# A decode kernel of two attention layers: six more V blocks kept in PSUM between the layers, and a new order in layer 2

## The chip, the cores and the metric

The kernel runs on one core of a Trainium2 chip. Its engines are TensorE (PE, whose weight loads are listed as PEld), VectorE (DVE), ScalarE (ACT), GpSimd (POOL) and SyncE (SP, which here only issues DMAs); 16 DMA engines carry the transfers. SBUF is the on-chip memory that DMAs fill; PSUM is the memory that TensorE writes, eight banks of 512 float32 words a partition here. The metric is the device time of one execution in microseconds (us). A second table is the hardware profiler's record of one execution of the same program.

## What is computed

One token (`x`, 640 values) goes twice through the same two blocks, A (attention) and B (an MLP with mixing), with the same weights and the same caches both times:

```python
x = x + A(layernorm(x));  x = x + B(layernorm(x))      # layer 1
x = x + A(layernorm(x));  x = x + B(layernorm(x))      # layer 2

def A(x):                       # 32 heads of 192, the last W = 4096 rows of each cache
    q = x @ wq
    p = softmax(q @ k.T * 192 ** -0.5)       # per head, [4096]
    return (p @ v) @ wo

def B(x):                       # one position: the shifted parts are zero
    return x + gelu(layernorm(x) @ w3) @ w4
```

With one position, the shifts in B push their content out, so that `w1` and `w2` have no effect on the result. K and V of a head are 4096 x 192 in bfloat16, 1536 KB each. Both layers use the same K, V and `wo`.

## The kernel before

**Cells.** Head data lives in twelve cells of SBUF, each 6144 bfloat16 words on 128 partitions, one K or V of a head. `take` (L147) hands out the cell that has been free longest, `give` (L152) returns one. A load into a cell waits until its last user is done, so the order of `give` sets when SP can issue which load. A V is 32 blocks of 192 words a partition, each block one key position a partition.

**The stream.** `layer_stream` (L247) writes down the loads of a layer in order; `need` issues them up to the one asked for. For each group of four heads the stream has K of the next group and V of the current one in turn, then `wo` of an earlier group; at the end of a layer come w3 and w4. All loads go through SP's queue, each of them also waiting for the eighth before it to land.

**What is kept for layer 2.** Layer 1 takes the groups from the last heads to the first. So the heads 0 to 7 come last and the transposed K of these eight stay in their cells (`kept`), as do V 3 (`VC`) and `wo` 0. V 2 (`VP`) is kept in pieces: 20 blocks are moved by `v_words` (L629) with VectorE transposes into four banks of PSUM (`V_bank`), since no cell is free, and moved back in layer 2 when one is; the other 12 blocks lie behind `wo` 0 in its cell. Of V 4 (`VX`), 24 blocks lie in the two spare areas `kl` and `kx`, so that layer 2 loads only 8 of its 32 blocks, 384 KB. `v_pair` (L185) tells where a pair of blocks lies.

**The work of a group** (`attention`, L720). VectorE transposes K in four quarters (`transpose_quart`, L433; `T` asks for two), TensorE makes scores (`scores`, L524, `S`). For a whole group the softmax runs in steps (`softmax_steps`, L551): maximum, turn, exponentials on ScalarE, `turn_p` on VectorE, `swap` on TensorE, which turns the probabilities into a PSUM tile and ScalarE copies them to `PT`. `pv` (L639) multiplies with V into `O_ps` and VectorE transposes the result; `o_fold` sums it up. `out_proj` or `out_row` (L670, L687) apply `wo` of the group before, `qproj_steps` make the next group's queries. The order of instructions on PE, DVE, ACT and SP is the order in which this code calls them (`manual_schedule`).

**Small results** (sums, turned maxima, queries) go to tiles of the pool `psm`, two PSUM banks in turn, each tile one bank; `ps` of the new version takes over this call. `mixer` (L963) makes block B, its 12 columns of hidden values in a free part of `V_bank` and of `O_bank` (`h_ps`).

Of the kernel before, what the change touches and what calls it, by code (L numbers as in the profile page):

```python
# [59 lines left out]
def kernel(  # L60
# [46 lines left out]
    VC, VP, VX, VW, VN = 3, 2, 4, 20 * Dh // 2, (NKL + NKX) * Dh  # L107
# [21 lines left out]
    psV = ctx.enter_context(tc.tile_pool(name="psV", bufs=1, space=PSUM))  # L129

# [38 lines left out]
    def load_v(layer, h):  # L169
        t = take(("v", layer, h))  # L170
        src = A_v_cache[0, h, s0:Sk, :].rearrange("(p j) d -> p (j d)", p=P)
        cut = (2 * VW,) if h == VP else (FREE - VN, FREE - NKX * Dh) if h == VX else ()
        if h in GROUPS[layer][-1][-1 - layer:]:
            cut = FREE // 2,
        i = 0
        for e in cut + (FREE,):
            kept_v = h == VP or h == VX and i > 0
            if not cut:
                load(t[:], src, layer == 0 or h >= 2)
            elif layer == 0 or not kept_v:  # L180
                nc.sync.dma_start(v_pair(t, h, i, e - i), src[:, i:e])
            i = e
        return t

    def v_pair(V, h, i, n):  # L185

        if h == VP and i >= 2 * VW:
            V, i = loaded["wo", 0, 0], i - 2 * VW + NA * D
        elif h == VX and i >= FREE - NKX * Dh:
            V, i = kx, i - (FREE - NKX * Dh)  # L190
        elif h == VX and i >= FREE - VN:
            V, i = kl, i - (FREE - VN)
        return V[:, i:i + n]

# [184 lines left out]
    warm_ps = psm.tile([32, 32], F32, tag="psm")  # L379
# [6 lines left out]
    xT_ps = psm.tile([P, ND], F32, tag="psm")  # L386
# [6 lines left out]
    def ln_center(x, rowsum):  # L393

        mean_ps = psm.tile([P, 1], F32, tag="psm")
# [11 lines left out]
        def total():  # L407
            var_ps = psm.tile([P, 1], F32, tag="psm")
            nc.tensor.matmul(var_ps[:], lhsT=ones, rhs=ssq[:, 0:1], start=True, stop=True)
            return var_ps  # L410
# [44 lines left out]
    def qproj_steps(c, xc, part=None, row=None):  # L455
# [6 lines left out]
        def project():  # L462
            need("wq", 0, ND - 1)
            if row is not None:
                N = QC // 2
                qr_ps = psm.tile([33, N], F32, tag="psm")
# [9 lines left out]
            qT_ps = psm.tile([P, n], F32, tag="psm")  # L476
# [8 lines left out]
        def spread():  # L485
            if row is not None:
                qT_ps = psm.tile([P, n], F32, tag="psm")
                for tl in range(n):
                    i, j = divmod(tl, n // 2)
                    nc.tensor.matmul(qT_ps[:, tl:tl + 1], lhsT=row[:, j * P:(j + 1) * P],  # L490
                                     rhs=Eq[0:33, i, 0:1], start=True, stop=True)
                held["q"] = qT_ps
# [6 lines left out]
        def repeat():  # L499
            Qrep_ps = psm.tile([P, 4 * n], F32, tag="psm")  # L500
# [50 lines left out]
    def softmax_steps(n, ST_ps, sc, space):  # L551
# [8 lines left out]
        def turn_max():  # L560
            pmT_ps = psm.tile([1, P], F32, tag="psm")
# [16 lines left out]
        def spread_max():  # L578
            nb_ps = psm.tile([P, 1], F32, tag="psm")
# [16 lines left out]
        def swap():  # L596
            ng = NGK // NT
            PT_ps = psm.tile([P, n, NJ4, NGK], F32, tag="psm")
# [7 lines left out]
            l_ps = psm.tile([P, QH], F32, tag="psm")  # L606
# [20 lines left out]
    h_ps = V_bank[:, VW:VW + NF // 2], O_bank[:, 2 * Dh:2 * Dh + NF // 2]  # L627

    def v_words(layer):  # L629

        V = need("v", layer, VP)
        step = 512
        for i in range(0, VW, step):
            n = min(step, VW - i)
            a = V[:, 2 * i:2 * (i + n)].bitcast(U32)
            b = V_bank[:, i:i + n].bitcast(U32)
            nc.vector.transpose(b if layer == 0 else a, a if layer == 0 else b)

    def pv(layer, h, hq, PT, mid=None):  # L639
        V = need("v", layer, h)  # L640
        if (layer, h) == (0, VP):
            v_words(0)
# [10 lines left out]
        else:  # L653
            give(("v", layer, h))
        nc.vector.transpose(o_sb[:], O_ps.rearrange("p (e a c) -> p e c a", e=2, c=NA))  # L655

    def o_fold(h, oT, rl, add=False):
        r = slice(32 * (h % QH), 32 * (h % QH) + 32)
        oT_ps = psm.tile([P, NA], F32, tag="psm")
# [10 lines left out]
    def out_proj(layer, *terms):  # L670

        y_ps = psm.tile([P, ND], F32, tag="psm")
# [14 lines left out]
    def out_row(layer, c, oT, acc, first):  # L687
# [3 lines left out]
        yr_ps = psm.tile([33, N], F32, tag="psm")  # L691
# [16 lines left out]
    def turn_row(acc):  # L708
        y_ps = psm.tile([P, ND], F32, tag="psm")
# [10 lines left out]
    def attention(layer, x_cur, rs_cur, x_new, z_new, rs_new, ss_new):  # L720
# [29 lines left out]
        def add_y(y_ps, n):  # L750
            y_new = x_new if n == 0 else short("y_acc", ND)
            if n == 1:
# [5 lines left out]
                def center():  # L758
                    nm_ps = psm.tile([P, 1], F32, tag="psm")
# [53 lines left out]
        for gi, cur in enumerate(groups):  # L813
# [6 lines left out]
            if nxt:  # L820
                part_max, turn_max, full_max, spread_max, turn_p, swap, recip = softmax_steps(len(cur), ST, sc, o_words)
# [24 lines left out]
                else:  # L846
# [18 lines left out]
                    in_row = gi - 1 in rows  # L865
                    if pending is not None:
                        y_ps = out_row(layer, *pending, acc, gi - 1 == rows[0]) if in_row else out_proj(layer, pending)
                    turn_p()
                    if quick:
                        y_ps()  # L870
# [4 lines left out]
                    if in_row:  # L875
                        if not quick:
                            y_ps()
                            if gi - 1 == rows[-1]:
                                add_y(turn_row(acc), 2)
# [4 lines left out]
                    PT = swap()  # L884
# [12 lines left out]
            for hq, h in order:  # L897
# [4 lines left out]
                elif quick and hq == 2:  # L902
                    T(h3, 1)
                pv(layer, h, hq, PT, steps[3] if quick and hq == 3 else fold)
# [17 lines left out]
                elif quick and hq == 2:  # L922
# [3 lines left out]
                    steps = softmax_steps(len(cur), ST_n, sc, kl[:].bitcast(F32))  # L926
# [36 lines left out]
    def mixer(layer, x_cur, z, rs_cur, ss_cur, x_new, rs_new):  # L963
# [4 lines left out]
        s1_ps = psm.tile([P, 1], F32, tag="psm")  # L968
        nc.tensor.matmul(s1_ps[:], lhsT=ones, rhs=rs_cur[:, 0:1], start=True, stop=True)
        s2_ps = psm.tile([P, 1], F32, tag="psm")  # L970
# [74 lines left out]
        y2_ps = psm.tile([P, ND], F32, tag="psm")  # L1045
# [26 lines left out]
    row_ps = psm.tile([ND, P], out.dtype, tag="psm")  # L1072
# [34 lines left out]
```

## Time and profile before

| | |
|---|---|
| median of three runs | 511.64 us (511.28 to 512.29) |
| the profiled execution, its time | 511.84 us |
| its span, first to last instruction | 509.9 us |
| busy: PE, DVE, ACT | 328.0, 292.0, 48.9 us |
| moved by DMA | 214.63 MB, 421 GB/s in the mean |
| K transposes (L450) | 224 of 943 ns |
| V products (L648) | 1000 recorded, 482 ns |
| V 2 into PSUM (L637) | 3 of 727 ns and 1 of 594 ns, from 270.8 us |
| V 2 back (L637) | 3 of 688 ns and 1 of 541 ns, from 295.1 us |

The span begins with the first instruction; about 285 us is the passage from layer 1 to layer 2. The times of groups are busy times of one engine; different engines work beside each other, so busy times do not add up to the span. "Idle before, releaser" names what ended an engine's idle time, and a chain entry for a DMA reaches from its issue to its landing, its time in the queue included.

### The profile page before, as it was taken

Reading aid. Unit: us, or ns where it says so; the run is one execution under the profiler, and the core shown is the slowest. Engines: PE = TensorE matmul, PEld = TensorE weight load, DVE = VectorE, ACT = ScalarE, POOL = GpSimd, SP = SyncE. Lnnn points to the kernel's source line nnn. Section 1 sums busy time; section 2 is a strip of 40 time slices with the busy share of each in tenths; the row PEclk is TensorE's granted clock in tenths of the full one; section 3 lists DMA queues with packets and bytes.
Section 4 is the critical chain, followed back from the end, with each engine's and each line's share of the span. In section 5 each row is a group of like instructions: output and inputs, shape, how many; then the busy total and the mean of one; then the engine's idle time right before and its main releaser. Section 6 shows DMA issues by size and latency. Waiting matters only on the chain.

```text
span 509.9 us, 9485 instructions
## 1 busy us (share of the span) xinstructions
PE 328.0 (64%) x4084; PEld 190.0 (37%) x4084; DVE 292.0 (57%) x604; ACT 48.9 (10%) x173; POOL 3.7 (1%) x16
## 2 busy tenths in 40 slices
PE   1057667677586675866665766658656765758685
PEld 0024333333343342533333643435333442434354
DVE  2077557657666656467624244756576566767522
ACT  1000101010010100101010100001010100101111
POOL 2000000000000000000000000000000000000000
PEclk9996666765756667577665585666786577886655
DMA  8999999999999999999999999999999999999996
GB/s 370 432 432 429 438 433 432 429 433 423 419 423 445 432 418 449 428 404 459 429 392 414 377 439 424 435 429 437 429 422 437 432 422 433 426 433 429 419 408 242
DMA packets 12015, 214.63 MB, mean 421 GB/s; under 512 B 2565, under 2 KB 3077, under 8 KB 7429
## 3 DMA queue, kind: packets, MB, share of 16 engines
q1 hardware_dynamic: 11972, 214.02, 98.5%
q8 instruction: 32, 0.52, 0.4%
q14 instruction: 11, 0.08, 0.0%
HBM read 214.01 MB, written 0.00 MB: 420 GB/s over the span
## 4 chain that ended last, share of the span: by engine, by line
DMA 42%; PE 28%; DVE 24%; issue 4%; ACT 1%; SPq 1%; DVEq 0%; ACTq 0%
DMA cell<-in_A_k_cache_dram 24%; DVE cell L450 17%; DMA cell<-in_A_v_cache_dram 14%; PE ST_ps L534 11%; PE O_ps L648 9%; DMA cell<-in_B_w_dram 4%; DVE o_sb L655 2%; PE qr_ps L469 2%; PE nb_ps L580 1%; PE yr_ps L694 1%; DVE words L557 1%; DVE o_sb L591 1%; PE l_ps L607 1%; PE y_ps L1051 1%; PE PT_ps L602 1%
## 5 line engine op out<-in xcount | busy, mean ns | idle before, releaser
L534 PE MATMUL ST_ps<-cell,Qblk 128*16 128x256 bf16 x1536 | 157.0, 364 | 101.6 <-DVE cell L450 69.1
L450 DVE STREAM_TRANSPOSE cell<-cell 128x768 uint32<-128x768 uint32 x224 | 200.3, 943 | 5.8 <-DMA cell<-in_A_k_cache_dram 5.4
L534 PEld LDWEIGHTS <-Qblk 128*16 128x16 bf16 x1536 | 82.8, 108 | 170.8 <-issue 146.9
L648 PE MATMUL O_ps<-cell,PT 128*2 128x384 bf16 x1000 | 103.1, 482 | 9.3 <-DMA cell<-in_A_v_cache_dram 7.4
L655 DVE STREAM_TRANSPOSE o_sb<-O_ps 128x384 f32<-128x384 f32 x64 | 37.2, 581 | 110.4 <-PE O_ps L648 110.3
L648 PEld LDWEIGHTS <-PT 128*2 128x2 bf16 x1024 | 46.1, 102 | 24.7 <-issue 15.7
L591 DVE STREAM_TRANSPOSE o_sb<-o_sb 128x256 bf16<-128x256 bf16 x15 | 6.7, 445 | 33.1 <-ACT o_sb L586 26.1
L663 ACT ACTIVATE words<-oT_ps,words 32x6 bf16<-32x6 f32 x40 | 10.3, 257 | 159.5 <-PE oT_ps L662 148.5
L662 PE MATMUL oT_ps<-o_sb,Lq 128*32 128x6 f32 x160 | 13.8, 195 | 10.4 <-DVE o_sb L655 9.8
L662 PEld LDWEIGHTS oT_ps<-o_sb,Lq 128*32 128x32 f32 x160 | 12.6, 143 | 20.4 <-issue 15.1
L668 ACT ACTIVATE words<-oT_ps,words 32x6 bf16<-32x6 f32 x24 | 6.2, 257 | 111.8 <-PE ST_ps L534 96.3
L480 PE MATMUL qT_ps<-words,wq_sb 128*128 128x1 bf16 x210 | 7.1, 165 | 12.8 <-DMA wq_sb<-in_A_wq_dram 11.9
L694 PE MATMUL yr_ps<-cell,words 128*1 128x320 bf16 x108 | 14.8, 439 | 0.0
L469 PE MATMUL qr_ps<-wq_sb,words 128*1 128x384 bf16 x90 | 14.2, 471 | 0.0
L494 DVE TENSOR_TENSOR o_sb<-qT_ps,words 128x24 bf16<-128x24 f32 (+1 forms) x18 | 3.0, 166 | 18.9 <-PE qT_ps L480 17.1
L480 PEld LDWEIGHTS <-wq_sb 128*128 128x128 bf16 x210 | 6.7, 102 | 14.0 <-DMA wq_sb<-in_A_wq_dram 13.0
L602 PE MATMUL PT_ps<-o_sb,ident 128*32 128x32 bf16 x240 | 6.8, 237 | 7.7 <-DVE o_sb L591 2.6
L607 PE MATMUL l_ps<-o_sb,words 128*128 128x4 f32 x30 | 7.8, 331 | 5.3 <-ACT PT L605 5.3
L602 PEld LDWEIGHTS <-ident 128*32 128x32 bf16 x256 | 5.6, 113 | 14.4 <-issue 14.1
L583 ACT COPY o_sb<-nb_ps 128x1 f32<-128x1 f32 x15 | 2.4, 159 | 88.6 <-PE nb_ps L580 88.6
L667 PE MATMUL oT_ps<-o_sb,Lq 128*32 128x6 f32 x48 | 6.0, 199 | 6.1 <-DVE o_sb L666 6.1
L667 PEld LDWEIGHTS oT_ps<-o_sb,Lq 128*32 128x32 f32 x48 | 5.7, 142 | 10.4 <-issue 9.9
(153 smaller groups left out, 202.0 us busy)
## 6 DMA issues: line engine op xcount, KB each, us to landing
cell<-in_A_k_cache_dram SPq DMA_DIRECT2D x56, 1536.0 KB, 25.6
cell<-in_A_v_cache_dram SPq DMA_DIRECT2D x56, 1536.0 KB, 26.3
cell<-in_A_wo_dram SPq DMA_DIRECT2D x13, 960.0 KB, 23.1
wq_sb<-in_A_wq_dram SPq DMA_DIRECT2D x5, 1536.0 KB, 13.4
cell<-in_A_v_cache_dram SPq DMA_DIRECT2D x6, 768.0 KB, 23.7
cell<-in_B_w_dram SPq DMA_DIRECT2D x1, 1536.0 KB, 11.8
cell<-in_B_w_dram SPq DMA_DIRECT2D x2, 768.0 KB, 10.3
cell<-in_A_wo_dram SPq DMA_DIRECT2D x3, 480.0 KB, 17.0
```

Of the source, the lines that this page charges most:

```text
L450: nc.vector.transpose(Tu, Ku[:, :, q * NY:(q + 1) * NY])
L469: nc.tensor.matmul(qr_ps[32 * i:32 * i + 1, :], lhsT=xc[:, kc:kc + 1], rhs=wq_sb[:, kc, t0 * P + i * N:t0 * P + (i + 1) * N], start=(kc == ...
L480: nc.tensor.matmul(qT_ps[:, tl:tl + 1], lhsT=wq_sb[:, kc, t * P:(t + 1) * P], rhs=xc[:, kc:kc + 1], start=(kc == 0), stop=(kc == ND - 1))
L534: nc.tensor.matmul(ST_ps[r:r + QW, :].rearrange("p (g i) -> p g i", g=ng), lhsT=Q[n], rhs=T4[:, :, f, :, t], start=(hq == 0 and n == 0), s ...
L591: nc.vector.transpose(held["PrT"], held["Pr"])
L602: nc.tensor.matmul(PT_ps[32 * m:32 * (m + 1), :, :, ng * q:ng * (q + 1)], lhsT=Eq[:, q, :], rhs=src[:, m:QW:NM], start=True, stop=True)
L607: nc.tensor.matmul(l_ps[:], lhsT=ones, rhs=held["lh"][:], start=True, stop=True)
L648: nc.tensor.matmul(O_ps[r:r + 2, :], lhsT=PT[:, hq, 2 * i:2 * i + 2], rhs=v_pair(V, h, 2 * i * Dh, 2 * Dh), start=(i < 4), stop=(i >= NB - 4))
L655: nc.vector.transpose(o_sb[:], O_ps.rearrange("p (e a c) -> p e c a", e=2, c=NA))
L662: nc.tensor.matmul(oT_ps[r, :], lhsT=Lq[:], rhs=o_sb[:, e, :, e], start=(e == 0), stop=(e == 1))
L667: nc.tensor.matmul(oT_ps[r, :], lhsT=Lq[:], rhs=o2, start=True, stop=True)
L694: nc.tensor.matmul(yr_ps[32 * i:32 * i + 1, :], lhsT=oT[:, k:k + 1], rhs=wo_t[:, k * D + i * N:k * D + (i + 1) * N], start=(k == 0), stop= ...
```

## The change

- **V 1's last six blocks** (`VQ`, `VR`) are moved by two transposes into PSUM before V 1's products in layer 1: 512 words a partition into a fifth bank (`v_rest`, one of `psm`'s two) and 64 into the rest of `V_bank`. In layer 2 they go back with V 2's blocks, into the free end of V 2's cell. Layer 2's V 1 is loaded without them.
- **Quarters.** While `v_rest` holds words, the other bank of `psm` (`work`) is cut into four parts of 128 words, and `ps` gives these in turn.
- **V 4.** Layer 2 loads six of V 4's blocks into the place of V 1's six in V 1's cell (a second transfer for that cell), and only two blocks, 96 KB, into V 4's own cell. V 1's cell is given back after V 4's products, not after V 1's.
- **Order in layer 2.** From the second group on, `swap` writes to `V_bank` (its first bank, and `l_ps` to its second). In every group whose steps run through this branch, `turn_p` and `swap` come ahead of the output projection; row sums are added after the next K's first half is transposed. For the second and third head of most groups, the first half of the next K is transposed ahead of the head's products and of the transpose of their result.
- `h_ps` lies at the end of `V_bank`'s fourth bank.

```diff
-    VC, VP, VX, VW, VN = 3, 2, 4, 20 * Dh // 2, (NKL + NKX) * Dh
+    VC, VP, VX, VQ = 3, 2, 4, 1
+    VW, VN, VR = 20 * Dh // 2, (NKL + NKX) * Dh, 6 * Dh
...
+    quarter = []
+    def ps(shape, dtype):
+        if not quarter:
+            return psm.tile(shape, dtype, tag="psm", name="psm")
+        quarter.append(quarter.pop(0))
+        t = quarter[-1]
+        if len(shape) == 2:
+            return t[0:shape[0], 0:shape[1]]
+        n, j, g = shape[1:]
+        return t[0:shape[0], 0:n * j * g].rearrange("p (n j g) -> p n j g", j=j, g=g)
...
-        cut = (2 * VW,) if h == VP else (FREE - VN, FREE - NKX * Dh) if h == VX else ()
+        cut = {VP: (2 * VW,), VX: (FREE - VN - layer * VR, FREE - NKX * Dh),
+               VQ: (FREE - VR,) * layer}.get(h, ())
...
-            kept_v = h == VP or h == VX and i > 0
+            kept_v = h == VP or h in (VX, VQ) and i > 0
...
+            elif h == VQ:
+                src = A_v_cache[0, VX, s0:Sk, :].rearrange("(p j) d -> p (j d)", p=P)
+                nc.sync.dma_start(t[:, i:e], src[:, FREE - VN - VR:FREE - VN])
...
+        elif h == VX and i >= FREE - VN - VR and ("v", 1, VQ) in loaded:
+            V, i = loaded["v", 1, VQ], i + VN
+        elif h == VQ and i >= FREE - VR and ("v", 1, VP) in loaded:
+            V, i = loaded["v", 1, VP], i - (FREE - VR) + 2 * VW
...
-    h_ps = V_bank[:, VW:VW + NF // 2], O_bank[:, 2 * Dh:2 * Dh + NF // 2]
+    h_ps = V_bank[:, 2048 - NF // 2:], O_bank[:, 2 * Dh:2 * Dh + NF // 2]
+    VB = 512
+    v_rest = []
...
+    def v_words(layer, h=VP):
+        V = need("v", layer, h)
+        if layer == 0 and h == VQ:
+            v_rest.append(psm.tile([P, VB], F32, tag="psm", name="v_rest"))
+            work = psm.tile([P, 512], F32, tag="psm")
+            quarter.extend(work[:, i:i + P] for i in range(0, 512, P))
+        if h == VP:
+            move_words(V, 0, V_bank[:, 0:VW], layer == 1)
+        if h == VQ or layer == 1:
+            i = 2 * VW if layer == 1 else FREE - VR
+            move_words(V, i, v_rest[0][:, :], layer == 1)
+            move_words(V, i + 2 * VB, V_bank[:, VW:VW + VR // 2 - VB], layer == 1)
+        if layer == 1:
+            quarter.clear()
...
-        else:
+        elif (layer, h) != (1, VQ):
             give(("v", layer, h))
+        if (layer, h) == (1, VX):
+            give(("v", 1, VQ))
...
+                    len(cur), ST, sc, o_words, V_bank if layer == 1 and gi > 0 else None)
...
+                    if layer == 1:
+                        turn_p()
+                        PT = swap()
                     if pending is not None:
                         y_ps = out_row(layer, *pending, acc, gi - 1 == rows[0]) if in_row else out_proj(layer, pending)
-                    turn_p()
-                    if quick:
-                        y_ps()
+                    if layer == 0:
+                        turn_p()
                     T(h1, 0)
...
-                    PT = swap()
+                    if layer == 0:
+                        PT = swap()
                     T(h1, 1)
...
+                elif layer == 1 and nxt and 0 < hq < 3:
+                    T(nxt[0][1], 0)
                 pv(layer, h, hq, PT, steps[3] if quick and hq == 3 else fold)
```

Layers are 0 and 1 in the code, 1 and 2 in the text. `move_words` holds the transposes that `v_words` had.

## The prediction

> **What bounds the kernel now.** I read the page's busy table, its slices and the chain first, then the stretches between the two layers, then what the DMA queue (SP) waits for.
>
> ```profile
> PE 328.0 (64%) x4084; PEld 190.0 (37%) x4084; DVE 292.0 (57%) x604; ACT 48.9 (10%) x173; POOL 3.7 (1%) x16
> ...
> DMA  8999999999999999999999999999999999999996
> GB/s 370 432 432 429 438 433 432 429 433 423 419 423 445 432 418 449 428 404 459 429 392 414 377 439 424 435 429 437 429 422 437 432 422 433 426 433 429 419 408 242
> ...
> DMA 42%; PE 28%; DVE 24%; issue 4%; ACT 1%; SPq 1%; DVEq 0%; ACTq 0%
> ```
>
> No engine is busy more than 64%; the 16 DMA engines are full in every slice but the first and the last. 214.0 MB go through them. The chain's 42% DMA understates this, because it follows a transfer back only to its issue, and the release that issued it is often an engine's. By stretches (columns: PE, PEld, DVE, ACT, POOL busy, clock, DMA share, GB/s):
>
> ```profile
> 282.00:284.00 2.00, 0.21 (x8) 0.22 (x9) 1.60 (x12) 1.09 (x5) 0.00 (x0) 0.50 0.96 328
> 284.00:287.00 3.00, 2.48 (x70) 2.31 (x68) 0.50 (x5) 0.14 (x2) 0.00 (x0) 0.50 1.01 419
> 291.00:295.00 4.00, 3.70 (x113) 2.94 (x117) 0.66 (x4) 0.46 (x2) 0.00 (x0) 1.00 0.92 326
> 304.00:354.00 50.00, 34.85 (x450) 19.97 (x446) 29.75 (x57) 5.15 (x18) 0.71 (x2) 0.60 1.00 430
> 404.00:454.00 50.00, 34.04 (x419) 19.02 (x418) 33.31 (x58) 5.62 (x19) 0.00 (x0) 0.77 1.00 430
> 500.00:503.00 3.00, 2.09 (x40) 1.93 (x40) 0.89 (x8) 0.73 (x4) 0.00 (x0) 0.50 1.01 399
> ```
>
> Layer 2's rate is flat at 430 GB/s. It is lower only around 282 to 295 us, where layer 2's first loads are issued late, and in the small pieces at the end. The issues there (SP's timeline):
>
> ```profile
> 281.70 3.80 SPq L156 DMA_DIRECT2D cell<-in_A_v_cache_dram  x2
> 289.51 0.33 SPq L156 DMA_DIRECT2D cell<-in_A_k_cache_dram  x1
> 291.02 0.33 SPq L181 DMA_DIRECT2D cell<-in_A_v_cache_dram  x1
> 292.12 0.48 SPq L55 DMA_DIRECT2D cell<-in_A_k_cache_dram  x1
> ```
>
> V 0 waits for the cell of w3, V 1 (issued at 285.18) for that of w4, K 8 for the first kept head's scores. From 304 on there is always a queue. SP's waits from 300 to 441 us, and then its longest from 441 to 503 us:
>
> ```profile
> SPq L55 <- PE O_ps L648: 35.9, 19, 5.6
> SPq L55 <- DVE cell L450: 11.0, 4, 3.5
> ...
> SPq L208 <- DMA cell<-in_A_v_cache_dram: 14.6, 5, 3.3
> SPq L181 <- DMA cell<-in_A_k_cache_dram: 9.6, 3, 3.3
> ```
>
> At first SP waits for cells that compute frees, yet loads still land 14 to 16 us after issue (four of 3.66 us: 1.573 MB at 430 GB/s). Later it waits for its own earlier transfers, with about seven in flight (25.6 us is the page's median from issue to landing of a K). Compute needs 28 to 29 us for a group (first K transposes at 312.65, 341.9, 371.3, 399.9 and 428.2); the group's 13.57 MB take 31.6 us. So compute, 15 us behind at 312, catches up with the data, and the stream sets the end: w3's second half lands at 503.10 and its matmuls run at 503.14.
>
> **The change, part by part.**
>
> *Bytes.* Layer 2 no longer loads V 1's last six blocks; V 4's six go into that place of V 1's cell, and V 4's own load falls from 384 KB to 96 KB. That is 288 KB, 294,912 bytes. At 430 GB/s it is 0.69 us. The load was issued at 291.02, K 9's behind it at 292.12, and K 9 landed at 302.4, a queue of 10 us: the place in the queue is real, and all behind it moves up. It is the only part on the path.
>
> *One more transfer.* V 1's load becomes two, of 9,984 and 2,304 bytes a partition. SP spends 0.33 us on one such issue; it would be idle from 285.5 to 289.5 anyway. The small piece is paid at the rate of the w4 pieces of 2,560 bytes, 399 GB/s against 430: 0.74 instead of 0.69 us, so 0.05 lost. The 96 KB in pieces of 768 bytes have no row; at worst they cost what the whole 384 KB did (0.91 us at 430) and nothing is gained, at best 0.23. I take 0.25, as rates fall slowly with size here (412 GB/s at 3,072 bytes, 399 at 2,560). Sum: 0.05 + 0.02 - 0.69 = -0.62 us. Ends: +0.05 and -0.69.
>
> The Trainium skill (DMA: Bandwidth & Descriptors, Anatomy of one DMA) gives a fixed cost of about 2.0 us per DMA, in a fit for GpSimd's path. By that figure the extra transfer would make the sum +1.4 us, an estimate from the page. The trace disagrees for transfers in a queue: 1.573 MB pieces follow each other at 3.66 us, with nothing between.
>
> *Saving V 1's blocks in layer 1.* Two more transposes before V 1's products. The row of 128x512 into PSUM has 0.73 us; 128x64 lies between a 0.16 us small instruction and 128x384's 0.59, and the line through the two rows gives 0.26. They start with the data, as the products do (266.24), and end at 267.2. The products end at 267.69 and w3's issue is at 267.73: hidden by 0.5 us. Without that cover w3 would be issued later, behind V 2 and V 3, which occupy the DMA engines until about 272. The banks that they and the quarters take were read last at 264.7 (DVE) and 265.1 (ACT): no wait.
>
> *Moving them back.* After V 2's four transposes (295.05 to 297.43), 0.69 and, on the same line, 0.17 us: DVE ends at 298.3. Behind it stands the maximum at 298.87, which waits for scores: 0.5 us of cover. Without it the first softmax of layer 2 would be up to 0.9 us later, inside compute's 15 us.
>
> *Quarters of one bank.* From V 1's products to the return of the blocks, four small places turn instead of two. The path from w4's last products to K 8's issue (285.66 to 289.51) shows only hand-offs of 0.26 to 0.28 us from engine to engine, no wait for a bank: 0, with -0.3 to +0.3 (one hand-off less or more). It counts, because no queue covers K 8's issue.
>
> *New order in layer 2.* Probabilities are turned ahead of the output projection, into banks of their own; two heads in a group get half of the next K's transposes ahead of O's. In the first such group (312 to 342) the turn moves from 321.86 to 319.8, V 4's products from 323.2 to about 322, and the projection's end from 320.0 to 321.8. Two waits of PE on K's transposes (1.54 us each at 329.18 and 336.01) shrink. At most 1.2 + 2 x 1.54 = 4.3 us a group, at least none. It costs or brings 0 at the end: compute catches up earlier and then waits for data. What comes next: DVE then stands before a K not yet landed, with O's transpose, the fold and the next products behind it. K lands 3.66 us after the V before it, so this is at most 3.66 us a head, inside the 31.6 us that the data take. POOL's two clears of kx wait for V 4's products and come as much earlier as these; nothing else stands in POOL's queue, and the order of the loads in SP's queue stays.
>
> *Cells.* V 1's cell is free only after V 4's products (about 323), not after its own (309.71). So wo 1, K 12, V 8, K 13 and V 9 each take a cell freed one step later: wo 1 at 311.8, K 12 at 316.5, V 8 (wo 0's cell) at 321.8. At 321.8 the load ahead, K 12, lands at about 326.8; an issue needs some 1.7 us to its first packet (K 8's start). Slack 3.3 us: 0.
>
> **Sum.** The profiled execution took 511.84 us (span 509.9, 1.9 around it), 0.20 above the median of 511.64. 511.84 - 0.62 = 511.22; on the median's footing 511.02.
>
> **The rivals.**
>
> *The hole before K 8 closes too.* From 291 to 295 us 326 of 430 GB/s were moved: 4 x (1 - 326/430) = 0.97 us lost. If the quarters' freer places, or a higher clock than 0.50, issue K 8 earlier, some returns: half gives 510.5, all 510.05. Against it: no bank wait is seen there.
>
> *The bytes fall into a hole.* If K 9 could not follow, V 4's place stays empty: 511.6 to 511.7. Against it: K 9's 10 us in the queue.
>
> *The extra transfer is paid.* If V 1's second piece holds K 8 up, then by the hole above up to 0.97 us: 512.0. Against it: K 8 is issued 4 us after V 1 and does not wait for its landing. (By the Trainium skill's 2.0 us, DMA: Bandwidth & Descriptors, Anatomy of one DMA, it would be 513.0; the flat 430 speaks against that.)
>
> *Slower: cells too late.* If wo 0's cell is freed more than 3.3 us after 321.8 (the turn or the projection stalls behind DVE), the stream stops, and each further microsecond costs one. It takes 0.62 + 1.02 = 1.64 us of emptiness to be slower by 0.2%: release after 326.7; 3 us of emptiness gives 514.0. For it: queue depth is lowest there. Against: it needs 5 us.
>
> **How the numbers follow.** 0.2% is 1.02 us, about what a measurement of this kernel tells from none. Forecast 0.59, own range 510.7 to 511.4; hole closes 0.20; bytes into a hole 0.05; extra transfer paid 0.06; cells too late 0.10. The hole closing needs half of its price to pass 0.2% and most of it does (0.17); 0.10 of the forecast's own may measure past it. Faster 0.27; slower: 0.10 and a third of 0.06, 0.12; same 0.61. The range goes from the hole closed, 510.0, to the extra transfer paid, 512.0.
>
> **What would show it.** Bytes 213.7 MB; V 4's load 96 KB at L196; 430 GB/s from 304 on with no slice below; K 9 landing some 0.6 us earlier against its issue; the end of w3 and the last product earlier by the same. In layer 2, waits of PE on K's transposes shrink and SP waits for DMA sooner. Wrong if K 8's issue moves against w4's landing, or if the rate dips between 320 and 335 us.

## The result, and the profile after

The changed kernel took 513.25 us (median of 12 executions, 511.84 to 513.78); the kernel before, on the same chip, 511.51 us (12 executions, 511.28 to 512.29). The ratio is 1.0027, 95% interval 1.0020 to 1.0034: slower by 1.7 us, where 0.6 us less was forecast. The times after also scatter over 2 us, those before over 1. The traced execution took 513.55 us, span 511.8, 1.71 us more than that of before. All times below are read against these traces unless a median is named.

The page of the changed kernel: the busy table, the slices of DMA share and rate, the chain.

```profile
PE 307.7 (60%) x4084; PEld 182.6 (36%) x4084; DVE 294.0 (57%) x608; ACT 48.9 (10%) x173; POOL 3.7 (1%) x16
...
DMA  8999999999999999999999999999999999999994
GB/s 369 430 430 428 428 447 426 439 428 415 455 428 416 446 412 425 432 410 452 432 393 416 389 425 433 424 428 432 425 409 457 428 420 434 422 433 432 415 411 178
...
HBM read 213.71 MB, written 0.00 MB: 418 GB/s over the span
...
DMA 64%; PE 18%; DVE 13%; issue 3%; ACT 1%; SPq 1%; DVEq 0%; ACTq 0%
```

The bytes are down as announced, the chain is DMA for 64% instead of 42%, and still the end is later. The slices that changed are few: the rate in the last one is 178 instead of 242 GB/s. By stretches (columns: PE, PEld, DVE, ACT, POOL busy, clock, DMA share, GB/s):

```profile
282.00:284.00 2.00, 0.61 (x23) 0.53 (x21) 1.14 (x9) 0.84 (x4) 0.00 (x0) 0.50 0.88 295
284.00:287.00 3.00, 2.38 (x62) 2.18 (x62) 0.90 (x7) 0.32 (x2) 0.00 (x0) 0.50 1.02 424
291.00:295.00 4.00, 3.75 (x97) 2.57 (x89) 0.55 (x4) 0.47 (x2) 0.00 (x0) 0.87 1.01 378
304.00:354.00 50.00, 36.62 (x543) 22.15 (x543) 36.74 (x71) 5.67 (x20) 0.71 (x2) 0.71 0.99 420
324.00:328.00 4.00, 3.59 (x60) 2.54 (x53) 3.96 (x11) 0.26 (x1) 0.52 (x2) 0.73 0.97 363
404.00:454.00 50.00, 28.85 (x346) 15.71 (x344) 29.34 (x51) 3.82 (x13) 0.00 (x0) 0.78 1.00 430
500.00:503.00 3.00, 2.35 (x40) 2.06 (x40) 0.88 (x10) 0.30 (x2) 0.00 (x0) 0.50 1.00 393
```

Three things stand out. From 282 to 284 us the rate is 295 (328 before). From 291 to 295 it is better, 378 (326 before); the kernel with the quarters alone, which moves the bytes of before, shows the same 378 there, so this isn't the work of the piece added to V 1, and what it comes from is not shown. And there is a new dip at 324 to 328 us, 363 GB/s, where before has 434:

```profile
324.00:328.00 4.00, 3.64 (x56) 2.19 (x45) 0.90 (x2) 0.26 (x1) 0.71 (x2) 0.50 1.02 434
```

SP's issues between the layers in the changed kernel (its timeline):

```profile
282.22 0.33 SPq L170 DMA_DIRECT2D cell<-in_A_v_cache_dram  x1
285.57 0.33 SPq L196 DMA_DIRECT2D cell<-in_A_v_cache_dram  x1
...
290.26 0.33 SPq L170 DMA_DIRECT2D cell<-in_A_k_cache_dram  x1
291.77 0.33 SPq L196 DMA_DIRECT2D cell<-in_A_v_cache_dram  x1
293.04 0.48 SPq L55 DMA_DIRECT2D cell<-in_A_k_cache_dram  x1
```

V 0 is issued 0.52 us later than before, V 1 0.39, K 8 0.75. The two waits behind it are in VectorE's timeline, after and then before:

```profile
280.55 0.17 DVE L1024 SCALAR_TENSOR_TENSOR words<-work,words 128x5 bf16<-128x5 f32 x1 [1.11 <-PE work L1021]
...
288.09 0.17 DVE L516 TENSOR_TENSOR o_sb<-work,words 128x12 bf16<-128x12 f32 x1 [1.03 <-PE work L502]
```

```profile
280.00 0.17 DVE L974 SCALAR_TENSOR_TENSOR words<-s_ps,words 128x5 bf16<-128x5 f32 x1 [0.61 <-PE s_ps L969]
...
287.33 0.17 DVE L494 TENSOR_TENSOR o_sb<-qT_ps,words 128x12 bf16<-128x12 f32 x1 [0.56 <-PE qT_ps L480]
```

Before, the first centring reads the first sum as soon as L969 has written it. After, it stands until L1021, the *second* sum, is done, although it doesn't read that one: both lie in quarters of one bank, `work`. The spreading of the first half of the query projection likewise waits for both halves. So 0.5 us and 0.47 us of waits appear that no operand asks for. (The Trainium skill, PSUM — Partial Sum Buffer, section "PSUM bank collisions raise a hardware error", has the rule that PSUM is to be guarded by bank and not by address. The trace is in line with it: different columns of one bank, and VectorE waits.) All quarters are views of one tile, though, and no run puts two tiles into one bank, so whether the wait is set for the bank or for the tile isn't shown.

The other end of the change is in the chain of waits in order of time, after and then before (start, us, what):

```profile
470.87 23.67 DMA cell<-in_A_v_cache_dram
494.54 0.02 issue
494.56 10.35 DMA cell<-in_B_w_dram
504.90 0.05 issue
504.95 0.49 PE V_ps L1054 x12
...
506.93 1.86 PE psm L1101 x60
```

```profile
469.12 23.66 DMA cell<-in_A_v_cache_dram
492.77 0.02 issue
492.79 10.31 DMA cell<-in_B_w_dram
503.10 0.05 issue
503.14 0.49 PE V_ps L1004 x12
...
505.12 1.92 PE y_ps L1051 x60
```

From the last but one half V on (the expectations call the last half V, at 492.32 in the mean, the last whole V), everything is the same length and 1.8 us later. The bytes do not explain it: there are fewer.

**Two clocks for a transfer.** The trace has the start, duration and size of each packet, but doesn't name which of the 16 DMA engines took it. Adding up the bytes in the order of the issues tells when the engines *on average* are done with a transfer. Its landing tells when the *slowest* is. For K 9 the mean is done at 301.2 us before and 300.5 after, which is 0.7 us earlier, the bytes' credit. It lands at 302.40 before and at 305.23 after. The slowest engine is 1.2 us behind the mean before, and 4.8 after. From there to the end the distance stays between 3.6 and 4.8 us in this trace: at the last half V the mean is done at 492.50 before and 492.32 after, and it lands at 494.63 and 496.38: distances 2.14 and 4.05. The 1.75 us between the landings is the difference of the kernels. (The Trainium skill, DMA: Bandwidth & Descriptors, section "Why a DMA increments its semaphore by 16 and not by 1", says that the engines finish independently and that only the last one's signal means landed; the numbers here are of that kind.)

The mean itself, counted by the bytes still to come, was 0.58 us ahead of before at 280 us, 0.71 at 304, 0.72 at 324, but 0.16 at 328: the dip takes 0.56 us of the credit. Counted in this way, the 0.69 us of saved bytes are ahead from the start; by the bytes moved, the changed kernel was 0.10 us behind at 280 and level at 304. The dip is measured by this loss from here on, since the rate of a 4 us window counts a packet where it starts and scatters: 397, 408 and 385 GB/s in three kernels whose mean loses 0.05 us at most there, 459 in a trace that loses 0.27 us.

SP's waits from 300 to 441 us, and then its longest from 441 to 503 us, show the forecast side effect: it waits for transfers early on instead of for cells.

```profile
SPq L55 <- DMA cell<-in_A_k_cache_dram: 39.6, 13, 4.8
SPq L55 <- DMA cell<-in_A_v_cache_dram: 34.8, 13, 3.1
SPq L55 <- PE O_ps L691: 20.1, 9, 5.6
...
SPq L230 <- DMA cell<-in_A_v_cache_dram: 14.6, 5, 3.3
SPq L196 <- DMA cell<-in_A_k_cache_dram: 9.7, 3, 3.3
```

### The profile page after: what moved, and what is told of

It is laid out like the page before. It is cut to its first block, busy times and chain, and to the rows that moved or that the text cites. A ratio compares the mean times of both kernels' runs of the same rounds, so it can differ in the third digit from the quotient of the medians.

```text
span 511.8 us, 9506 instructions
## 1 busy us (share of the span) xinstructions
PE 307.7 (60%) x4084; PEld 182.6 (36%) x4084; DVE 294.0 (57%) x608; ACT 48.9 (10%) x173; POOL 3.7 (1%) x16
## 4 chain that ended last, share of the span: by engine, by line
DMA 64%; PE 18%; DVE 13%; issue 3%; ACT 1%; SPq 1%; DVEq 0%; ACTq 0%
DMA cell<-in_A_k_cache_dram 37%; DMA cell<-in_A_v_cache_dram 24%; DVE cell L472 8%; PE ST_ps L556 7%; PE O_ps L691 5%; DMA cell<-in_B_w_dram 2%; DVE o_sb L700 2%; PE psm L602 1%; PE psm L635 1%; DVE o_sb L613 1%; PE psm L502 1%; DVE words L579 1%; PE psm L721 1%; PE psm L627 0%; SPq L55 0%
## 5 line engine op out<-in xcount | busy, mean ns | idle before, releaser
L691 PE MATMUL O_ps<-cell,PT 128*2 128x384 bf16 x1000 | 86.4, 422 | 13.2 <-DMA cell<-in_A_v_cache_dram 11.9
L691 PEld LDWEIGHTS <-PT 128*2 128x2 bf16 x1024 | 39.5, 94 | 29.1 <-issue 19.8
L708 ACT ACTIVATE words<-psm,words 32x6 bf16<-32x6 f32 x37 | 9.5, 257 | 152.7 <-PE psm L707 139.8
L707 PE MATMUL psm<-o_sb,Lq 128*32 128x6 f32 x148 | 12.1, 190 | 9.8 <-DVE o_sb L700 9.3
L707 PEld LDWEIGHTS psm<-o_sb,Lq 128*32 128x32 f32 x148 | 10.3, 133 | 19.0 <-issue 13.0
L713 ACT ACTIVATE words<-psm,words 32x6 bf16<-32x6 f32 x24 | 6.2, 257 | 106.1 <-PE ST_ps L556 78.6
L516 DVE TENSOR_TENSOR o_sb<-psm,words 128x24 bf16<-128x24 f32 (+1 forms) x15 | 2.4, 161 | 19.1 <-PE psm L502 15.8
L502 PE MATMUL psm<-words,wq_sb 128*128 128x1 bf16 x150 | 5.4, 166 | 12.7 <-DMA wq_sb<-in_A_wq_dram 12.1
L491 PE MATMUL psm<-wq_sb,words 128*1 128x384 bf16 x90 | 11.0, 387 | 0.0
L739 PE MATMUL psm<-cell,words 128*1 128x320 bf16 x108 | 10.4, 336 | 0.0
L712 PE MATMUL psm<-o_sb,Lq 128*32 128x6 f32 x48 | 5.8, 193 | 6.9 <-DVE o_sb L711 6.9
L602 PEld LDWEIGHTS psm<-words,o_sb 1*128 1x128 f32 x30 | 7.0, 290 | 7.0 <-issue 5.3
L602 PE MATMUL psm<-words,o_sb 1*128 1x1 f32 x30 | 8.3, 343 | 1.5 <-DVE o_sb L594 1.5
L712 PEld LDWEIGHTS psm<-o_sb,Lq 128*32 128x32 f32 x48 | 5.0, 133 | 11.0 <-issue 8.8
```

Source lines behind the costliest of these rows:

```text
L491: nc.tensor.matmul(qr_ps[32 * i:32 * i + 1, :], lhsT=xc[:, kc:kc + 1], rhs=wq_sb[:, kc, t0 * P + i * N:t0 * P + (i + 1) * N], start=(kc == ...
L502: nc.tensor.matmul(qT_ps[:, tl:tl + 1], lhsT=wq_sb[:, kc, t * P:(t + 1) * P], rhs=xc[:, kc:kc + 1], start=(kc == 0), stop=(kc == ND - 1))
L602: nc.tensor.matmul(nb_ps[:], lhsT=held["w"], rhs=one[0:1, :], start=True, stop=True)
L691: nc.tensor.matmul(O_ps[r:r + 2, :], lhsT=PT[:, hq, 2 * i:2 * i + 2], rhs=v_pair(V, h, 2 * i * Dh, 2 * Dh), start=(i < 4), stop=(i >= NB - 4))
L707: nc.tensor.matmul(oT_ps[r, :], lhsT=Lq[:], rhs=o_sb[:, e, :, e], start=(e == 0), stop=(e == 1))
L708: nc.scalar.activation(oT[r, :], oT_ps[r, :], ACTF.Copy, scale=rl[r, 0:1])
```

## The experiments

**The parts one by one.** First the new order of layer 2 alone, in the kernel before (the probabilities go to V_ps's banks, as in the change):

```diff
+                    if layer == 1:
+                        turn_p()
+                        PT = swap()
                     if pending is not None:
                         y_ps = out_row(layer, *pending, acc, gi - 1 == rows[0]) if in_row else out_proj(layer, pending)
-                    turn_p()
+                    if layer == 0:
+                        turn_p()
...
+                elif layer == 1 and nxt and 0 < hq < 3:
+                    T(nxt[0][1], 0)
                 pv(layer, h, hq, PT, steps[3] if quick and hq == 3 else fold)
```

> The kernel before with only the new order of layer 2 (probabilities turned and swapped ahead of the projection, into banks of V_ps; half of the next K's transposes ahead of a head's O). No byte and no transfer changes, and nothing changes between the layers. Theory (the new order only lets compute catch up earlier): within 0.4 us of before, 511.1 to 511.9; K 8 issued at 289.5 and K 9 landed at 302.4 as before, and waits of SP for transfers start well before 441 us. Rival (the new order is what costs the 1.7 us of the whole change): 513.0 to 513.5. Rival (emptiness near 325 us comes from the new order): the rate in 324 to 328 us drops below 400 GB/s here too.

Measured: 511.68 us against 511.56, ratio 1.0002 (0.9994 to 1.0011). K 8 issued at 289.58, K 9 landed at 303.01. The window from 324 to 328 us reads 385 GB/s, under the 400 that the rival named, but the bytes moved lose only 0.01 us there: no dip. The order alone costs nothing and brings nothing.

Then the changed kernel with layer 2 in its old order (the same edit taken back):

> The changed kernel with layer 2 in its old order; all else (V 1's six blocks, the quarters, V 4's blocks in V 1's cell) stays. Theory (the time is lost between the layers, where one DMA engine falls behind the others by up to 4.8 us and stays behind to the end): 513.0 +- 0.5, the quarters' waits still there, K 8 issued at 290.2 and K 9 landed after 304.5. Rival (the new order is what costs): 510.8 to 511.2. Rival (V 1's cell held too long is what costs): the cells come one step later here too and the old order frees them later still, so 513.5 or more, with a dip of the rate between 320 and 335 us.

Measured: 512.81 us, ratio 1.0022 (1.0013 to 1.0032). K 8 issued at 290.26, as expected; K 9 landed at 301.89, which was not. The dip between 324 and 328 us is there too, 0.63 us in the mean. So neither the loss nor the dip is the order's. Whether the order adds the 0.44 us between this and the changed kernel is not resolved: the intervals overlap.

The quarters alone, in the kernel before (every small result goes through the change's `ps`, and the quarters end with the return of V 2's words):

```diff
+        if (layer, h) == (0, 1):
+            work = psm.tile([P, 512], F32, tag="psm", name="work")
+            quarter.extend(work[:, i:i + P] for i in range(0, 512, P))
...
-            nm_ps = psm.tile([P, 1], F32, tag="psm")
+            nm_ps = ps([P, 1], F32)
```

> The kernel before with only the small results in quarters of one bank from V 1's products in layer 1 to the return of V 2's words in layer 2; no byte, no transfer, no order changes. Theory (the shared bank makes VectorE wait for sums and projections that it does not read): V 0 issued 0.5 us and K 8 0.7 us later against w4's landing than before, 512.0 to 512.4 if this emptiness is paid in full, and 513 or more if it also sets one DMA engine behind the rest. Rival (the small transfers set the engine behind): K 8 late by the same 0.7 us, but the last transfer's landing stays within 1 us of before. Rival (the quarters cost nothing, as predicted): 511.3 to 511.8 and K 8 issued at 289.5.

Measured: 512.93 us against 511.56, ratio 1.0023 (1.0014 to 1.0033). V 0 issued at 282.26, K 8 at 290.30, and the distance of the slowest engine 3.85 us at the last half V. With no byte, transfer or order changed, this one edit costs 1.37 us. The small transfers as the cause of the distance fall here: this kernel has none, and the distance all the same.

The 288 KB taken off V 1's own load, so that no transfer is added and no cell is held:

```diff
-        cut = {VP: (2 * VW,), VX: (FREE - VN - layer * VR, FREE - NKX * Dh),
+        cut = {VP: (2 * VW,), VX: (FREE - VN, FREE - NKX * Dh),
...
-            elif h == VQ:
-                src = A_v_cache[0, VX, s0:Sk, :].rearrange("(p j) d -> p (j d)", p=P)
-                nc.sync.dma_start(t[:, i:e], src[:, FREE - VN - VR:FREE - VN])
...
-        if (layer, h) == (1, VX):
-            give(("v", 1, VQ))
```

> The changed kernel, but the 288 KB come off V 1's own load: V 1 is one transfer of 9,984 bytes a partition, V 4's remains 3,072 bytes a partition in a cell of its own, and V 1's cell is given after V 1's products. So no transfer is added, none has pieces of 768 or 2,304 bytes, and no cell is held longer; the same 288 KB less are moved. Theory (the two small transfers set one DMA engine behind): the gap between the slowest engine and the mean stays near 2 us, no dip at 324 to 328 us, 510.8 to 511.5. Rival (the quarters' late K 8 sets it behind): the gap grows to over 4 us all the same, the dip is gone, 512.3 to 513.0. Rival (only the held cell costs): 0.6 us below the changed kernel.

Measured: 513.16 us, ratio 1.0029 (1.0018 to 1.0040), a little above the rival's range. V 0 at 282.33, K 8 at 290.36. The dip is gone: in the trace the mean keeps its place within 0.1 us from 304 to 332. So the dip belongs to the held cell or the added transfer, which this edit takes away together; but the quarters' cost is all still here. The gap was 2.6 us in this trace, not over 4. Instead the mean fell from 0.53 us ahead of before at 280 us to 0.32 behind at 304: here the loss lies mostly in the stream as a whole, around the late issues.

**The waits taken away.** The second sum and the second half of the projection go to unused columns of O_ps's bank, in the changed kernel:

```diff
-        s2_ps = ps([P, 1], F32)
+        s2_ps = O_bank[:, 400:401] if layer == 0 else ps([P, 1], F32)
...
-            qT_ps = ps([P, n], F32)
+            qT_ps = O_bank[:, 404:404 + n] if quarter and part == 1 else ps([P, n], F32)
```

> The changed kernel with two of its small results between the layers put elsewhere: the second sum and the second half of the first query projection go to unused columns of O_ps's bank instead of quarters of the shared one. Theory (the shared bank is the cause): VectorE no longer waits for them, V 0 issued at 281.7 and K 8 at 289.6 to 289.7, the gap of the slowest DMA engine to the mean near 2 us at the end; the 0.69 us of bytes less the 0.6 us of the emptiness at 324 us stay: 511.2 to 511.8. Rival (the small transfers of 768 and 2,304 bytes): 512.8 to 513.4, as the changed kernel.

Measured: 511.53 us against 511.49, ratio 1.0005 (0.999 to 1.002). VectorE starts the centring at 280.15, and SP's issues are back (its timeline):

```profile
281.85 0.33 SPq L170 DMA_DIRECT2D cell<-in_A_v_cache_dram  x1
...
289.61 0.33 SPq L170 DMA_DIRECT2D cell<-in_A_k_cache_dram  x1
```

The distance at the last half V is 2.29 us. Two small results in another bank take 1.7 us off the changed kernel (513.25 and 511.53 were taken on two chips, whose kernels before took 511.51 and 511.49): the quarters' waits are the loss. The order, the bytes, the added transfer and the held cell together come to nothing that the interval, half a us down and one up, can tell.

The same two results elsewhere, with the 288 KB off V 1's own load:

> The same two results put elsewhere, in the kernel that takes the 288 KB off V 1's own load (no added transfer, no cell held longer). Theory: V 0 and K 8 issued as before, no emptiness at 324 us, so the bytes are earned: 510.7 to 511.2. Rival (without the small second piece of V 1 nothing fills the time from V 1's end to K 8's first packet, so the 0.69 us fall into a hole there): 511.4 to 511.8.

Measured: 511.15 us against 511.49, ratio 0.9990 (0.9981 to 0.9998). This is 0.1% faster than the kernel before. The page of this kernel:

```profile
GB/s 371 432 432 430 430 441 432 422 434 426 417 427 441 432 423 449 432 398 439 434 403 412 379 422 432 439 426 434 430 423 447 430 418 430 427 439 426 423 403 245
```

Its last slice moves 245 GB/s, like before's 242. In the trace the mean, counted by the bytes still to come, is 0.57 us ahead at 280 us and 0.49 at 304, and about there to the end, so the emptiness before K 8 takes little of the bytes.

Which of the two waits? One at a time, in the kernel with quarters alone. The second sum elsewhere:

```diff
-        s2_ps = ps([P, 1], F32)
+        s2_ps = O_bank[:, 400:401] if layer == 0 else ps([P, 1], F32)
```

> The kernel before with quarters, with the second sum alone put elsewhere: V 0 issued at 281.7 again, K 8 still 0.6 to 0.8 us late. Theory (K 8's late issue is what costs): 512.7 to 513.1, the slowest engine's gap still over 3.5 us. Rival (V 0's late issue is what costs): 511.4 to 511.8 and a gap near 2 us.

And the second half of the projection elsewhere:

```diff
-            qT_ps = ps([P, n], F32)
+            qT_ps = O_bank[:, 404:404 + n] if quarter and part == 1 else ps([P, n], F32)
```

> The kernel before with quarters, with the second half of the first query projection alone put elsewhere: K 8 issued at 289.6 to 289.7, V 0 still 0.5 us late. Theory (K 8's late issue is what costs): 511.4 to 511.8 and a gap near 2 us. Rival (V 0's late issue is what costs): 512.7 to 513.1, the gap over 3.5 us.

Measured: with the sum elsewhere 511.58 us (ratio 1.0001, 0.9992 to 1.0011); with the projection elsewhere 512.23 (1.0012, 1.0003 to 1.0020). VectorE's waits in the first and then in the second of these kernels:

```profile
DVE o_sb L507 <- PE work L493: 1.0, 1, 1.0
DVE words L992 <- PE work L987: 0.7, 1, 0.7
```

```profile
DVE words L992 <- PE work L989: 1.1, 1, 1.1
DVE o_sb L507 <- PE work L493: 0.6, 1, 0.6
```

My theory, that K 8's late issue is what costs, fell as stated: by the medians the wait ahead of V 0 is the dearer one, though the two intervals overlap. The second kernel met neither range, and K 8 wasn't on time in it either: it was issued at 290.07, 6.14 us after w4's landing (5.77 before), where 289.6 to 289.7 was expected. So the wait ahead of V 0 makes both issues late. Each kernel had a small distance (1.95 and 2.20 us).

**The lateness without quarters.** In the kernel before, only the two sums in one bank, and then the second sum three times (the diff is the latter's; the former has one pass):

```diff
-        s1_ps = psm.tile([P, 1], F32, tag="psm")
-        s2_ps = psm.tile([P, 1], F32, tag="psm")
+        both = psm.tile([P, 4], F32, tag="psm", name="both")
+        s1_ps = both[:, 0:1] if layer == 0 else psm.tile([P, 1], F32, tag="psm", name="s1")
+        s2_ps = both[:, 1:2]
+        for j in range(3 if layer == 0 else 1):
+            nc.tensor.matmul(both[:, 1 + j:2 + j], lhsT=ones, rhs=ss_cur[:, 0:1], start=True, stop=True)
```

> The kernel before with one edit: the two sums ahead of layer 1's second half share one bank instead of having one each, so VectorE's first centring waits for the second sum. Theory (the late V 0 is the cost, whatever made it late): V 0 issued 0.5 us later, 512.0 to 512.4. Rival (the late V 0 costs only together with the rest of the quarters): 511.4 to 511.7.

> The same with the second sum run three times in that bank, the wait made longer: V 0 issued 1.0 to 1.6 us later than before. Theory: the emptiness at 282 to 285 us is paid in full or more, 512.7 to 513.5. Rival (lateness at this place is made up by the transfers behind it): at most 0.3 us above the kernel with one sum each.

Measured: 511.98 us against 511.58 (ratio 1.0010, 1.0001 to 1.0019), and 512.45 (1.0022, 1.0012 to 1.0033). Traces drift by 0.1 to 0.5 us ahead of this place, so the lateness is best taken from the layer's last addition on VectorE to V 0's issue: 2.55 us before, 2.94 with one bank, 3.79 with three sums, and 3.02 in the changed kernel. So 0.39 us of lateness costs 0.40, at the theory's lower edge, but 1.24 us only 0.87: between the theory's range and the rival's. With three sums K 8 is late as well, by 1.0 us (6.78 us after w4's landing), so the 0.87 is the price of both; with one bank K 8 is late by 0.08. The wait in the second kernel:

```profile
DVE words L976 <- PE both L973: 1.9, 1, 1.9
```

Quarters with both results elsewhere, nothing else:

> The kernel before with quarters and with both results put elsewhere; no byte changes. Theory: the quarters cost nothing when no engine waits for a neighbour's result: 511.3 to 511.7; against it the kernel with 288 KB less and the same two results elsewhere (511.15) tells what the bytes earn, 0.3 to 0.6 us. Rival (a further wait hides in the quarters): 512.0 or more.

Measured: 511.53 us against 511.58, ratio 1.0003 (0.9994 to 1.0012). There is no further wait in the quarters. By the medians the bytes are then worth some 0.4 us (511.15 against 511.53, on two chips), little more than half of their 0.69.

And K 8 late alone, with the projection's halves in one bank and the second half run twice:

```diff
-            qT_ps = psm.tile([P, n], F32, tag="psm")
-            for tl in range(n):
+            if bank is None:
+                qT_ps = psm.tile([P, n], F32, tag="psm", name="qT_ps")
+            else:
+                qT_ps = bank[:, part * n:(part + 1) * n]
+            for tl in list(range(n)) * (1 if bank is None or part == 0 else 2):
...
+        one_bank = psm.tile([P, QT], F32, tag="psm", name="one_bank") if layer == 1 else None
```

> The kernel before with the two halves of layer 2's first query projection in one bank and the second half run twice: V 0 issued as before, K 8 1.2 to 1.8 us later. Theory (K 8's late issue costs little, as 0.52 us of it cost 0.1 with the sum put elsewhere): up to 512.0. Rival (the emptiness before K 8 is paid in full once V 1's data run out, as the prediction had it: no queue covers K 8's issue): 512.7 to 513.3.

Measured: 512.05 us, ratio 1.0012 (1.0003 to 1.0021). From w4's landing to K 8's issue there are 6.58 us instead of 5.77, so 0.81 us of lateness rather than the 1.2 to 1.8 meant. Some of it is paid, about half by the medians, with a wide interval.

**What the excess is made of.** 0.47 us on V 0 and 0.64 on K 8 (from w4's landing) cost 1.4 to 1.7 us together. More traces of the changed kernel, of the quarters alone, and of the changed kernel with both results elsewhere were to tell whether that is the distance or an emptiness of the whole stream:

> The changed kernel once more, for a second execution with a trace. Theory (the time above the bytes' is the distance of the slowest DMA engine from the mean of the 16, which differs from execution to execution): the mean of the engines finishes the last whole V within 0.3 us of the first trace's 492.32, and the execution's time less the landing of that V stays 17.1 to 17.2 us, so that a time of 512.2 goes with a distance of about 2.7 and one of 513.6 with about 4.1. Rival (the emptiness in the stream itself differs): the distance stays near 4 us and the mean moves with the time.

> A third execution of the changed kernel with a trace: as the second.

> The kernel before with quarters alone, a second trace. Theory: the mean within 0.3 us of 492.44, the time 513.4 less 3.85 us plus this execution's distance. Rival: the distance near 3.9 again whatever the time.

> The changed kernel with the second sum and the second half of the query projection elsewhere, a second trace. Theory: a distance under 2.6 us and a time under 511.6 again, the mean within 0.3 us of 491.72; a time of 513 or more, as two of its twelve had, would come with a distance of 4 us.

Measured, each row one traced execution (the last half V: when the mean of the engines is done, the distance of the slowest, the landing; all us):

| kernel | time | mean done | distance | landed |
|---|---|---|---|---|
| before | 511.84 | 492.50 | 2.14 | 494.63 |
| changed, first trace | 513.55 | 492.32 | 4.05 | 496.38 |
| changed, second | 513.54 | 492.27 | 4.02 | 496.29 |
| changed, third | 513.82 | 492.98 | 3.69 | 496.67 |
| quarters alone, first | 513.37 | 492.44 | 3.85 | 496.29 |
| quarters alone, second | 513.23 | 492.68 | 3.48 | 496.16 |
| changed, both results elsewhere, first | 511.18 | 491.72 | 2.29 | 494.02 |
| changed, both results elsewhere, second | 512.63 | 493.08 | 2.26 | 495.34 |
| V 1 short, both results elsewhere | 511.07 | 491.92 | 1.87 | 493.80 |

The time less the landing is 17.1 to 17.3 us in all of these (of the other traces only the old order's is outside, with 17.9). Of the 18 traces that there are, seven have both waits; in five of them the distance is 3.5 to 4.1 us, in two (the old order, 2.3, and V 1 short, 2.6) it is not. In the eleven without both it is 1.9 to 2.4. So in the changed kernel's first two traces and in both of the quarters alone the stream as a whole is no later than before by more than 0.2 us, and one or more engines are; the kernel with V 1 short lost its time in the mean. Half of the expectation failed, though: the changed kernel's mean moves too, by 0.7 us between its traces, and the second trace of the kernel with both results elsewhere is 1.45 us slower at the same distance. There the dip took 0.99 us instead of 0.24, and the mean was 0.4 us later by 304 us already.

The packets say more about the engine behind. On one engine a packet starts 4 ns before the end of the one ahead, so packets can be strung into chains, one for each engine, without its name. The page counts one more user of these engines:

```profile
q8 instruction: 32, 0.52, 0.4%
```

These are 32 loads of instructions of 16 KB. In each of the 18 traces the 18th of them, begun between 301.7 and 306.3 us, fills a gap in one chain: in the changed kernel's first trace a packet of K 9 ends at 303.225, the load runs from 303.222 for 0.955 us, the next packet starts at 304.173 and takes 2.29 us, where most take 1.82. By these figures the load costs its engine some 1.4 us. In the five traces with a distance of 3.5 to 4.1 us this engine ended its part of K 9 1.3 to 2.8 us after the mean; in the other thirteen it was between 0.7 ahead and 0.8 behind. In the five it had also begun K 8 at 293.3 to 293.8 us with a first packet of 1.3 to 2.0 us, where 0.46 is usual. The loads are there before the change too; what differs is that they hit an engine that is late already.

The dip shows as a loss of the mean between 324 and 328 us in all six traces of kernels that hold V 1's cell (0.24 to 0.99 us), and in none of the twelve others (0.06 at most). It goes with V 8's issue: 0.24 and 0.27 us at 321.79 and 321.58, 0.56 to 0.64 at 321.98 to 322.67, 0.99 at 323.90; before, V 8 is issued at 316.52.

## Why the prediction was wrong

It was wrong in sign, and by more than its range. Step by step:

*Quarters of one bank* is the step that failed. It was costed at 0, -0.3 to +0.3, because the path of before showed only hand-offs, "no wait for a bank". That was read from a trace in which each result has a bank of its own, and could not show what sharing does. The right question was which instruction reads one quarter while TensorE still writes another; there are two, L1024 and L516, and each then waits for matmuls that it has no use for: the end of the wait moves by 0.55 us for the second sum and 0.76 for the second half of the projection. Even so, the sum of the two as lateness of the issues would be about 1.1 us; the kernel with the quarters alone lost 1.37, and taking the two waits out of the changed kernel returned 1.7. The step was also right on one thing, that no queue covers K 8's issue, but it missed that V 0's issue ahead of it is as bare: that wait is the dearer of the two by the medians (0.65 us between the kernels with one of them each, with intervals that overlap), and it makes K 8 late as well.

*Bytes* went as computed in the mean: by the bytes still to come it was 0.58 to 0.72 us ahead until 324 us. What it took for granted is that the end follows the mean. It follows the slowest engine. With the waits gone the bytes were worth 0.4 us by the medians.

*Cells* failed in part. K 12's landing was put at 326.8 us and V 8's slack at 3.3 us. V 8 was issued at 322.67, 0.9 late, and the dip came all the same, since the slack was counted to a landing, the slowest engine's end. K 12 landed at 329.16, but the mean engine was done with it at 325.0, and the fastest earlier still. Even with V 8 at 321.79, as forecast, 0.24 us went. The rival "cells too late" named the place and not the price: it needed a release after 326.7. The shift of the cells and the added transfer together cost 0.38 us by the medians (511.53 against 511.15, not clear of the noise); no run parts these two.

*One more transfer*: the 2.0 us by the Trainium skill's figure for a DMA's fixed cost (DMA: Bandwidth & Descriptors, Anatomy of one DMA) were not paid: with the held cell it is 0.38 us by the medians, and the dip alone took 0.24 and 0.99 of the mean in that kernel's two traces.

*Saving V 1's blocks* and *moving them back* held. The two transposes took 0.73 and 0.22 us at 266.26, and w3 was issued at 267.70 (267.73 before); the way back took 0.67 and 0.21, ending at 299.07, ahead of the maximum at 299.41.

*New order* held: 0 at the end, alone as well, and SP waits for transfers from the 350s on instead of the 440s. What the prediction named as its refutation, K 8's issue moving against w4's landing and a rate that dips between 320 and 335 us, both came.

What stays open: why, with both waits, one engine comes to K 8 late and slowly in 5 of 7 traces, and why the load of instructions then hits this one. The distance is shown, its link with both waits together by 5 of 7 against 0 of 11 traces, and that the load adds to it; the order by which loads and packets fall to the engines is not. The costs of the single waits do not add up exactly either: 0.1 and 0.7 us for the kernels with one wait, 1.4 for both, each with an interval of some 0.5 us either way.

## What to carry to other kernels

When small results are moved into one bank of PSUM, list for each reader which matmuls into the same bank stand between its producer and itself: those can now be waited for, as they were here, and a wait-free trace of before says nothing about it. In a kernel bound by DMA, put a result that nobody is in a hurry for next to one that everybody waits for only if both are written by then; a few unused columns in another bank did the job here. Count the slack of a transfer to the moment when the first DMA engine runs dry, not to the landing of the one ahead, and don't book saved bytes before checking that the issues at the places where the queue is empty stay where they were.

## What was not expected of the hardware

The 16 DMA engines drift apart and stay apart: the slowest was 1.9 to 2.4 us behind the mean at the end of all kernels without both waits, and up to 4.8 us behind right after K 9 in the changed one, 200 us before the end. It did not come back in the 200 us left: 4.75 us at K 9, 3.6 at 350 us, 4.05 at the last half V. Loads of instructions, 16 KB in some 0.95 us each, run on the same engines as the data, and one that hits the engine that is late already sets it further back, by some 1.4 us. The price of late issues doesn't follow their size: 1.24 us at V 0 together with 1.0 at K 8 cost 0.87, and 0.47 together with 0.64 cost 1.4.
